# Fills ahead of the counting products, and joined maxima, exponentials, query flips and w2 casts at later steps of the w1 product

## The chip, the core and the metric

One core of a Trainium2 chip runs the kernel. The metric is the device time of one execution in microseconds (us). Inputs and output lie in the chip's memory (HBM).

## The reference

For each of 8 batches, 8 heads attend in two stages: 32 packed queries `p` attend to 576 keys and values, and then the 576 queries `q` attend to the 32 packed rows. The result, 4608 rows of 512, goes through a mixture of 8 experts, of which each row takes the best.

```python
def _attn_ref(q, k, v, p):                       # q, k, v: (8, 8, 576, 64), p: (8, 8, 32, 64)
    p_packed = sm_attn(p, k, v)                  # softmax(p k' / 8) v, with 1e-9 on the sum
    return sm_attn(q, p_packed, p_packed)
...
    logits = xn @ en.T / tau                     # rows and expert embeddings, normalised
    expert_idx = np.argmax(logits, axis=1)
    for e in range(E):                           # w1: (8, 512, 1024), w2: (8, 1024, 512)
        mask = expert_idx == e
        h = np.maximum(x[mask] @ w1[e], 0.0)
        out[mask] = gate_w[mask, None] * (h @ w2[e])
```

## The kernel before

A batch is one unit of work. For the rows of a batch the kernel guesses one expert from the packed rows, runs the two products of that expert for all 576 rows, and counts afterwards whether every row did want it; rows that did not would go through a second part at the end of the program, which these inputs do not enter.

**Two streams are woven by hand.** `ffn(b)` is the expert of batch b and a generator that yields after each group of products on TensorE; a loop at the end of the program (`step_att`) then runs one step of `att_main(b + 1)`, the attention of the next batch. Every engine executes its instructions in the order in which they are written, so a step of the attention stands on each engine behind what `ffn` wrote ahead of the yield and in front of what it writes after it.

**The w1 product** is `hidden(hf, f)`: two halves of the 576 rows (hf) times eight blocks of 128 hidden columns (f), 16 units. Here they are called h0 to h15; h0 to h7 are the first half. Each writes one PSUM bank `pf`, of which there are three, in six products of 128x288, and yields. After the yield its bank is read twice: ScalarE writes the rounded ReLU (L982) and VectorE the remainder (L983, which reads ScalarE's result); in the second half VectorE also copies 64 columns into `h4` (L988). The bank is free when all of these are done, so h(n+3) waits for the readers of h(n). In the second half some units are followed by `split_w2`: a cast of one block of w2 on ScalarE (L886) and the subtraction of its remainder on GpSimd (L887).

**After the w1 product** come eight units of products with `h4` (L1013) and 32 units of the w2 product (L1031), which read `w2s`, the split blocks. With the first step behind the last `h4` unit the attention issues the query scores (L266), which read the four flipped query tiles.

**The attention of batch b+1**, for b+1 from 2 to 7, is `att1`'s `pack()`. Step n stands behind unit n. Before the change:

- Step 0: `counts` of batch b (two products with ones, L824 and L827, and a reduction on VectorE, L829); two fills of parts of the banks for the key scores (L319, VectorE); the key scores on TensorE (L325).
- Steps 1 and 2: `quarter_max` of the two halves of the heads (L337, VectorE).
- Step 3: `whole_max`, six small operations on VectorE (L345 to L351) that join the maxima of four row groups; the first two exponentials (L357, ScalarE).
- Steps 4 to 6: the other six exponentials, two in each. Steps 5 and 7: `quarter_flip`, two additions on GpSimd (L373) and a transpose of 128x640 on VectorE (L374).
- Steps 8 and 9: the first two query flips (L287, VectorE, 128x576).
- Step 12: the values (L384, L393, TensorE). Step 13: sums and scaled rows (L400 to L402, L476, VectorE). Step 14: `pair_turn` (L486, TensorE). Step 15: copy of `x.T` (L550) and the third query flip. Step 16: the fourth. Steps 17 and 18: `row_logits`, `logits_out` (L497, L506).
- Steps 19 to 22: `guess`: products (L610), the index of the largest on VectorE (L616 to L621), and its read by GpSimd, which then issues the loads of w1 and w2. Step 23: the query scores. Then the softmax of the second stage (L656 to L696, mostly VectorE) and `route`, both within the w2 product.
- From unit 18 on a step of `gates` of batch b (L92 to L108 and on, tiny operations of VectorE) follows each step.

**Loads.** Four buffers `nat` hold key and query tiles. A flip of tile i asks for the load of tile i+3; the values' step asks for all keys of the next batch but for those under way. These loads, the values' (`vn`, two buffers) and the stores of the output stand in one queue, that of SyncE, in program order.

Of the kernel before, what the change touches and what calls it, by code (L numbers as in the profile page):

```python
# [27 lines left out]
def kernel(  # L28
# [16 lines left out]
    NG = H // HB  # L45
# [203 lines left out]
    def idle(n):  # L249
        for _ in range(n):  # L250
            yield
# [56 lines left out]
    def area(x, g):  # L308
        t = x.s1[g].rearrange("p (f w) -> p f w", f=2)[:, :, : 2 * QW]
        return t.rearrange("p f (s k) -> p f s k", s=2)  # L310
# [1 line left out]
    def place(h):  # L312
        return h % 2 * 2 + h // 2

    def quarter_scores(x):

        for g in range(NG):
            x.s1[g] = pb.tile([P, 1024], F32, name="pt", tag="pb")
            nc.vector.memset(area(x, g)[64:P, :, :, :32], LOW)  # L319
        for r in range(NPR):  # L320
            for a in range(HB):
                at = RUNS[a] * 32 + (32 if a >= 2 else 0)
                n = QW - (32 if a >= 2 else 0)
                for u in range(2):
                    nc.tensor.matmul(  # L325
                        area(x, r // 2)[32 * a : 32 * a + 32, u, r % 2, QW - n :],
                        half_rows(x.pw, u)[:, r],
                        half_rows(x.kT[r], u)[:, at : at + n],
                        start=True,
                        stop=True,  # L330
                        tile_position=(64 * u, 32 * a),
                    )
# [152 lines left out]
    def pair_turn(x, g, pt):  # L485
        nc.tensor.transpose(  # L486
            pt[:, g * P : (g + 1) * P], pairs_of(x, g), ident
        )

    def pack_tiles(x):  # L490
        x.T = x.Tq = sm.tile([P, NG * P], F32, name="T", tag="T", bufs=1)
        x.ppx = sb.tile([P, NG, XW], F32, name="ppx", tag="ppx", bufs=2)
# [15 lines left out]
    def all_queries(x, nat):  # L508
        for r in range(NPR):
            x.qT[r] = flip(nat(NPR + r))  # L510
            yield

    def att1(x, nat):

        queries = all_queries(x, nat)

        def pack():
            pack_tiles(x)
            quarter_scores(x)
            yield  # L520
            quarter_max(x, 0)
            yield
            quarter_max(x, 1)
            yield
            whole_max(x)
            for g in range(NG):
                for n in range(HB):
                    quarter_exp(x, g, n)
                    if n % 2:
                        yield  # L530
                quarter_flip(x, g)
            yield
            for _ in range(2):
                next(queries)
                yield
            yield from idle(2)
            pt = pb.tile([P, 1024], F32, name="pt", tag="pb")
            sums = pt[:, NG * D : NG * D + NG * QW // 4].rearrange("p (g k) -> p g k", g=NG)
            for g in range(NG):
                quarter_values(x, g, nat(2 * NPR + g), pt[:, g * D : g * D + D], sums[:, g])  # L540
            yield
            quarter_sums(x, sums)
            for g in range(NG):
                pair_rows(x, g, pt[:, g * D : g * D + D])
            yield
            pu = pc.tile([P, 512], F32, name="pu", tag="pu")
            for g in range(NG):
                pair_turn(x, g, pu)
            yield
            nc.vector.tensor_copy(x.T, pu[:, 0 : NG * P])  # L550
            next(queries)
            yield
            next(queries)
            yield
            pt = pc.tile([P, 512], F32, name="pu", tag="pu")
            row_logits(x, pt)
            yield
            logits_out(x, pt)
            yield

        def pack_slowly():
            pack_tiles(x)
            for g in range(NG):
                pt = pb.tile([P, 1024], F32, name="pt", tag="pb")
                p1_turn(x, g, pt)
                yield
                p1_evac(x, g, pt)
                key_sum(x, g)
                yield
            pt = pb.tile([P, 1024], F32, name="pt", tag="pb")  # L570
            for g in range(NG):
                pack_values(x, g, nat(2 * NPR + g), pt[:, g * D : g * D + D])
            yield
            for g in range(NG):
                pair_rows(x, g, pt[:, g * D : g * D + D])
            yield
            pu = pc.tile([P, 512], F32, name="pu", tag="pu")
            yield
            for g in range(NG):
                pair_turn(x, g, pu)  # L580
            yield
            nc.vector.tensor_copy(x.T, pu[:, 0 : NG * P])
            yield
            pt = pc.tile([P, 512], F32, name="pu", tag="pu")
            row_logits(x, pt)
            logits_out(x, pt)
            yield

        if x.halves:
            for g in range(NG):  # L590
                key_max(x, g)
                yield
                key_exp(x, g)
                yield
            yield from pack_slowly()
        else:
            yield from pack()


    def guess(x, late=0, engine=mybir.EngineType.Pool, total=None):  # L600
# [329 lines left out]
    def ffn(x, store, late=False, after=None, end=False, between=None):  # L930
# [30 lines left out]
        def hidden(hf, f):  # L961
            cs = slice(hf * HS, (hf + 1) * HS)
            pf = ps.tile([P, 512], F32, name="pf", tag="pf")

            assert not late or hf == 0 or hf in x.lows and x.gs >= NG * (f // 4 + 1)
            if late and hf == 0:
                ops = [
                    (x.g32[f // 4][:, g, f % 4 * P : f % 4 * P + P], x.ats[0][:, g])
                    for g in range(NG)
                ]  # L970
            else:
                ops = [
                    (x.G[:, a, g, f * P : (f + 1) * P], x.AT[:, m, g, cs])
                    for g in range(NG)
                    for a, m in PASSES
                ]
            for n, (w, r) in enumerate(ops):
                nc.tensor.matmul(pf[:, :HS], w, r, start=(n == 0), stop=(n == len(ops) - 1))  # L978
            yield
            n = HS if hf == 0 else 512 - HS  # L980
            cs = slice(hf * HS, hf * HS + n)
            nc.scalar.activation(hT[:, 0, f, cs], pf[:, :n], AF.Relu)  # L982
            nc.vector.scalar_tensor_tensor(  # L983
                out=hT[:, 1, f, cs], in0=pf[:, :n], scalar=0.0,
                in1=hT[:, 0, f, cs].bitcast(F32), op0=ALU.max, op1=ALU.subtract,
            )
            if hf:
                nc.vector.tensor_scalar(  # L988
                    out=h4[:, f], in0=pf[:, n:HS], scalar1=0.0, scalar2=None, op0=ALU.max
                )  # L990
            if f % 2 and hf and not late:
                split_w2(x)

        if not late and not hasattr(x, "w1g"):
# [86 lines left out]
    def nat_main(b):  # L1081
        def get(i):
            if i < NKQ:
                prefetch(order[b, i] + 3)
                if b > 1 and i in (NPR - 1, NPR):
                    loaded[b, i + NPR + 1] = load_nat(b, i + NPR + 1)
            else:
                prefetch(order[b, NKQ - 1] + 4)
            return loaded[b, i]

        return get

    def att_main(b):
        x = bat[b]
        if b:
            if b > 1:
                counts(bat[b - 1])
            yield from att1(x, nat_main(b))
            sync = b == 1
            queue = nc.sync if sync else nc.gpsimd  # L1100
            yield from guess(
                x, 0 if sync else 2, mybir.EngineType.SP if sync else mybir.EngineType.Pool
            )
            load_w1(x, x.e, queue=queue)
        flips = keys_main(b + 1) if b else None
        second = att2(x, flips, b == 0, b < 1, ENG1 if b == 1 else "vvvvpv")
        if b:
            if b > 1:
                yield
            for _ in range(3 if b == 1 else 2):  # L1110
                yield next(second)
            load_w2(x, x.e, queue)
            if b == 1:
                yield from idle(3)
        yield from second
        x.soft = True
        if b:
            steps = {"r": route(x), "f": flips}
            if b == 1:
                next(flips)  # L1120
            for turn in TURNS:
                for step in turn:
                    next(steps[step], None)
                yield
        if b == B - 1:
            yield from idle(2)
            counts(x)
# [455 lines left out]
```

## Time and profile before

| what | us |
|---|---|
| median of three runs | 448.89 |
| lowest and highest run | 448.1 and 449.75 |
| time of the profiled execution | 449.35 |
| its span | 447.7 |
| TensorE busy | 422.2 |
| VectorE busy | 311.8 |
| ScalarE busy | 198.9 |
| GpSimd busy | 154.8 |

The span is from the first to the last instruction of the profiled execution; 1.65 us of its time lie around it. Matmuls are pipelined and their ends are modelled. In the timelines each line has the start, the length, the engine, the source line, the operation, the tiles and shapes and the number of instructions, and in brackets how long the engine had been idle and what ended that. The chain of waits is followed back from the last instruction.

### The profile page before, as it was taken

The numbers are of one execution on the slowest core, as the hardware profiler recorded it, in microseconds if no ns is written. First come the engines' busy times: TensorE is split into PE (matmuls) and PEld (weight loads), VectorE is DVE, ScalarE is ACT, GpSimd is POOL, SyncE is SP. The second block draws the span as 40 slices with busy tenths as digits, with TensorE's granted clock in tenths as the row PEclk, the third lists the DMA queues.
The fourth block names the chain that finished last, engine by engine and source line by source line (L and its number), as shares of the span: only waits on it lengthen the run. The fifth ranks groups of instructions, "written<-read, shape, count | busy, mean of one in ns | idle before, by whom it ended". The sixth has DMA issues, their size and how long they took to land.

```text
span 447.7 us, 11089 instructions
## 1 busy us (share of the span) xinstructions
PE 422.2 (94%) x4094; PEld 332.0 (74%) x4095; DVE 311.8 (70%) x930; ACT 198.9 (44%) x472; POOL 154.8 (35%) x177
## 2 busy tenths in 40 slices
PE   8899999989998999989999899998999899999993
PEld 5658677777867878678776778777786787769783
DVE  2677686578966789668876779677896588656500
ACT  3567615562264623654146522545236451466210
POOL 2244812445322551425314344034612255142200
PEclk9999999999999999999999999999999999999998
DMA  8899895876978488964979469785698805611012
GB/s 222 293 246 293 229 324 184 223 187 162 378 195 200 99 243 319 226 166 128 294 259 229 123 163 330 240 194 139 185 362 214 198 5 189 243 29 26 14 48 53
DMA packets 42223, 87.92 MB, mean 196 GB/s; under 512 B 11306, under 2 KB 20522, under 8 KB 42162
## 3 DMA queue, kind: packets, MB, share of 16 engines
q1 hardware_dynamic: 34896, 61.44, 51.2%
q0 software_dynamic: 6720, 25.17, 15.5%
q10 hardware_dynamic: 546, 0.54, 0.6%
q8 instruction: 34, 0.56, 0.5%
q14 instruction: 27, 0.22, 0.2%
HBM read 77.68 MB, written 9.44 MB: 195 GB/s over the span
## 4 chain that ended last, share of the span: by engine, by line
PE 86%; DVE 6%; ACT 2%; DMA 2%; issue 1%; SPq 0%; ACTq 0%
PE pf L1031 40%; PE pf L978 21%; PE pf L1013 6%; PE pt L746 5%; PE pt L911 3%; PE pt L266 2%; PE pt L384 2%; PE pt L325 2%; DMA nat<-in_k 2%; DVE hT L983 2%; PE pf L1171 1%; DVE qm L337 1%; ACT p L357 1%; ACT hT L982 1%; PE pu L610 1%
## 5 line engine op out<-in xcount | busy, mean ns | idle before, releaser
L1031 PE MATMUL pf<-w2s,hT 128*128 128x512 f32 (+1 forms) x792 | 183.9, 388 | 0.0
L1031 PEld LDWEIGHTS pf<-w2s,hT 128*128 128x128 f32 x792 | 143.1, 188 | 39.6 <-issue 10.7
L887 POOL TENSOR_TENSOR w2s<-w2r,w2s 128x512 fp32r<-128x512 f32 x64 | 81.6, 1286 | 121.3 <-ACT w2s L886 61.2
L978 PE MATMUL pf<-AT,G 128*128 128x288 f32 x720 | 109.9, 302 | 10.9 <-DVE hT L983 9.6
L978 PEld LDWEIGHTS pf<-AT,G 128*128 128x128 f32 x720 | 98.2, 188 | 20.2 <-DVE hT L983 13.4
L983 DVE SCALAR_TENSOR_TENSOR hT<-pf,hT 128x224 fp32r<-128x224 f32 (+1 forms) x128 | 52.5, 412 | 32.3 <-ACT hT L982 30.8
L982 ACT ACTIVATE hT<-pf 128x224 fp32r<-128x224 f32 (+1 forms) x128 | 49.5, 392 | 56.4 <-PE pf L978 55.1
L1372 ACT ACTIVATE o<-pf,gate 128x512 f32<-128x512 f32 (+1 forms) x41 | 25.9, 633 | 35.3 <-PE pf L1031 21.9
L886 ACT CAST w2s<-w2r 128x512 fp32r<-128x512 f32 x64 | 38.6, 616 | 0.0
L287 DVE STREAM_TRANSPOSE kt<-nat 128x576 f32<-128x576 f32 x52 | 37.9, 756 | 0.2 <-issue 0.2
L758 ACT ACTIVATE scr<-pt 128x512 f32<-128x512 f32 (+2 forms) x47 | 24.9, 531 | 24.7 <-PE pt L746 23.8
L1013 PE MATMUL pf<-w2r,h 128*64 128x256 f32 x256 | 33.8, 388 | 0.0
L373 POOL TENSOR_TENSOR qs<-p 128x320 f32<-128x320 f32 x12 | 10.6, 881 | 50.5 <-ACT p L357 50.5
L761 DVE TENSOR_REDUCE lg<-pt 128x8 f32<-128x32 f32 (+2 forms) x47 | 8.6, 182 | 27.7 <-ACT scr L758 27.5
L670 ACT ACTIVATE st<-st 128x576 f32<-128x576 f32 (+1 forms) x17 | 11.1, 658 | 34.4 <-DVE st L667 32.6
L746 PEld LDWEIGHTS pt<-ppx,at 64*128 64x128 f32 (+1 forms) x320 | 19.4, 175 | 7.1 <-issue 4.6
L746 PE MATMUL pt<-ppx,at 64*128 64x136 f32 (+1 forms) x320 | 24.3, 290 | 0.0
L696 POOL TENSOR_TENSOR AT<-at,AT 128x576 fp32r<-128x576 f32 x7 | 10.0, 1423 | 40.4 <-ACT AT L691 40.4
L1013 PEld LDWEIGHTS pf<-w2r,h 128*64 128x64 f32 x256 | 19.4, 137 | 4.9 <-issue 1.8
L357 ACT ACTIVATE p<-pt,qnm 128x160 f32<-128x160 f32 x48 | 16.9, 424 | 12.0 <-DVE qnm L351 12.0
L691 ACT CAST AT<-at 128x576 fp32r<-128x576 f32 x15 | 10.1, 674 | 22.7 <-DVE at L685 22.7
L849 ACT ACTIVATE lg<-lg 128x40 f32<-128x40 f32 x8 | 1.9, 237 | 40.8 <-DVE lg L845 40.8
(205 smaller groups left out, 484.2 us busy)
## 6 DMA issues: line engine op xcount, KB each, us to landing
nat<-in_q SPq DMA_DIRECT2D x112, 140.0 KB, 3.3
nat<-in_k SPq DMA_DIRECT2D x96, 140.0 KB, 2.9
w1t<-in_moe_w POOLq DMA_DIRECT2D x12, 1024.0 KB, 9.2
w2r<-in_moe_w POOLq DMA_DIRECT2D x24, 512.0 KB, 11.8
out<-o SPq DMA_DIRECT2D x124, 64.0 KB, 2.7
vn<-in_v SPq DMA_DIRECT2D x48, 160.0 KB, 4.2
w2r<-in_moe_w SPq DMA_DIRECT2D x8, 512.0 KB, 9.8
nat<-in_k SPq DMA_DIRECT2D x4, 576.0 KB, 7.2
```

The costliest lines, as they stand in the source:

```text
L287: nc.vector.transpose(kt.rearrange("p (c i) -> p c i", i=32), t)
L357: nc.scalar.activation(x.p1[g][:, n * QW : n * QW + QW], area(x, g)[:, n // 2, n % 2], AF.Exp, bias=x.nm[:, at : at + 1],)
L746: nc.tensor.matmul(to[: rows(c), half], x.at[at, g, c * P : c * P + rows(c)], x.ppx[at, g], start=True, stop=True, tile_position=(64 * hal ...
L758: nc.scalar.activation(scr[:r, :, : pt.shape[2]], pt[:r, :, :, : 2 * D], AF.Square, accum_out=sss[:r])
L886: nc.scalar.copy(t[:, 0], raw)
L887: nc.gpsimd.tensor_tensor(out=t[:, 1], in0=raw, in1=t[:, 0].bitcast(F32), op=ALU.subtract)
L978: nc.tensor.matmul(pf[:, :HS], w, r, start=(n == 0), stop=(n == len(ops) - 1))
L982: nc.scalar.activation(hT[:, 0, f, cs], pf[:, :n], AF.Relu)
L983: nc.vector.scalar_tensor_tensor(out=hT[:, 1, f, cs], in0=pf[:, :n], scalar=0.0, in1=hT[:, 0, f, cs].bitcast(F32), op0=ALU.max, op1=ALU.su ...
L1013: nc.tensor.matmul(pf[64 * hf : 64 * hf + 64, :256], h4[:, f], x.w2r[f // 2][:, f % 2, hf * 256 : hf * 256 + 256], start=(f == 0), stop=(f ...
L1031: nc.tensor.matmul(pf[:, :w], hT[:, a, f, c * P : (c + 1) * P], x.w2s[f][:, m, at : at + w], start=(f == 0 and i == 0), stop=(f == NF - 1 ...
L1372: nc.scalar.activation(o[:, :w], pf[:, :w], AF.Copy, scale=x.gate[:, c : c + 1])
```

## The change

The two fills move out of `quarter_scores` into `quarter_banks`, which is called ahead of `counts`. `whole_max` moves from step 3 to step 4, and two more empty steps follow it, so that the exponentials stand at steps 6 to 9 and the `quarter_flip` parts at steps 8 and 10. The four query flips stand at steps 12 (behind the values), 14, 18 (behind `logits_out`) and 20 (behind `guess`'s index). Of `split_w2` the four calls in the second half follow f = 4 to 7 (h12 to h15) instead of f = 1, 3, 5, 7 (h9, h11, h13, h15). The loads of the two value tiles are asked for by the third and fourth key flip instead of the fourth key flip and the first query flip. The step numbers of values, sums, `pair_turn`, copy, logits, guess and query scores stay.

```diff
-    def quarter_scores(x):
-
+    def quarter_banks(x):
         for g in range(NG):
             x.s1[g] = pb.tile([P, 1024], F32, name="pt", tag="pb")
             nc.vector.memset(area(x, g)[64:P, :, :, :32], LOW)
+
+    def quarter_scores(x):
...
-    def att1(x, nat):
-
-        queries = all_queries(x, nat)
-
-        def pack():
+    def att1(x, nat, queries=None):
+
+        def pack(queries):
             pack_tiles(x)
+            if not x.s1:
+                quarter_banks(x)
             quarter_scores(x)
             yield
-            quarter_max(x, 0)
-            yield
-            quarter_max(x, 1)
+            for g in range(NG):
+                quarter_max(x, g)
+                yield
             yield
             whole_max(x)
+            yield from idle(2)
             for g in range(NG):
                 for n in range(HB):
                     quarter_exp(x, g, n)
                     if n % 2:
                         yield
                 quarter_flip(x, g)
-            yield
-            for _ in range(2):
-                next(queries)
-                yield
             yield from idle(2)
...
                 quarter_values(x, g, nat(2 * NPR + g), pt[:, g * D : g * D + D], sums[:, g])
+            next(queries)
             yield
             quarter_sums(x, sums)
...
                 pair_turn(x, g, pu)
+            next(queries)
             yield
             nc.vector.tensor_copy(x.T, pu[:, 0 : NG * P])
-            next(queries)
-            yield
-            next(queries)
-            yield
+            yield from idle(2)
             pt = pc.tile([P, 512], F32, name="pu", tag="pu")
             row_logits(x, pt)
             yield
             logits_out(x, pt)
+            next(queries)
             yield
...
-            yield from pack()
+            asked = queries or all_queries(x, nat)
+            yield from pack(asked)
+            if queries is None:
+                drain(asked)
...
-            if f % 2 and hf and not late:
+            if f >= 4 and hf and not late:
                 split_w2(x)
...
-                if b > 1 and i in (NPR - 1, NPR):
-                    loaded[b, i + NPR + 1] = load_nat(b, i + NPR + 1)
+                if b > 1 and i in (NPR - 2, NPR - 1):
+                    loaded[b, i + NPR + 2] = load_nat(b, i + NPR + 2)
...
             if b > 1:
+                quarter_banks(x)
                 counts(bat[b - 1])
-            yield from att1(x, nat_main(b))
+            queries = all_queries(x, nat_main(b)) if b > 1 else None
+            yield from att1(x, nat_main(b), queries)
...
-            yield from guess(
+            for n, _ in enumerate(guess(
                 x, 0 if sync else 2, mybir.EngineType.SP if sync else mybir.EngineType.Pool
-            )
+            )):
+                if n == 1 and queries:
+                    next(queries)
+                yield
```

## Rows read from the trace of the kernel before

**Rows 1.** The page's busy times of the engines, with shares and instructions.
```profile
PE 422.2 (94%) x4094; PEld 332.0 (74%) x4095; DVE 311.8 (70%) x930; ACT 198.9 (44%) x472; POOL 154.8 (35%) x177
```
**Rows 2.** Chain of waits, whole run: start, length, engine, tile, line, instructions.
```profile
84.46 0.79 PE pf L978 x6
...
104.40 1.01 PE pf L1013 x8
...
295.87 0.79 PE pf L978 x6
...
315.81 1.01 PE pf L1013 x8
320.13 1.13 PE pt L266 x32
...
348.71 0.79 PE pf L978 x6
...
368.66 1.01 PE pf L1013 x8
...
402.06 12.71 PE pf L978 x96
```
**Rows 3.** Timeline of TensorE from 295 us: where it stood idle in one w1 product.
```profile
297.51 1.29 PE L325 MATMUL pt<-kt,pw 64*32 64x160 f32 x64 [0.57 <-DVE pt L319]
...
304.54 7.01 PE L978 MATMUL pf<-AT,G 128*128 128x288 f32 x42 [1.59 <-DVE hT L983]
```
**Rows 4.** Timeline of ScalarE, same stretch: the exponentials and a w2 cast.
```profile
303.01 0.68 ACT L357 ACTIVATE p<-pt,qnm 128x160 f32<-128x160 f32 x2 [2.00 <-DVE qnm L351]
...
308.66 0.61 ACT L886 CAST w2s<-w2r 128x512 fp32r<-128x512 f32 x1
```
**Rows 5.** Timeline of VectorE, same stretch: fills, joined maxima, flips, sums, logits, index.
```profile
297.20 0.30 DVE L319 MEMSET pt<- 64x128 f32 x2
...
301.85 0.17 DVE L345 COPY qlow<-qm 64x8 f32<-64x8 f32 x1
...
302.82 0.16 DVE L351 COPY qnm<-qnm 64x8 f32<-64x8 f32 x1
304.02 0.46 DVE L983 SCALAR_TENSOR_TENSOR hT<-pf,hT 128x288 fp32r<-128x288 f32 x1 [1.04 <-ACT hT L982]
...
305.27 0.83 DVE L374 STREAM_TRANSPOSE p1T<-p 128x640 f32<-128x640 f32 x1
...
308.10 0.76 DVE L287 STREAM_TRANSPOSE kt<-nat 128x576 f32<-128x576 f32 x1
...
313.07 0.24 DVE L400 TENSOR_REDUCE qr<-pt 128x2 f32<-128x80 f32 x1 [0.58 <-PE pt L393]
...
317.77 0.14 DVE L506 COPY ppx<-pu 128x16 f32<-128x16 f32 x1
317.82 0.27 DVE L92 TENSOR_SCALAR rq_i<-ss 128x5 int32<-128x5 int32 x1
...
319.51 0.22 DVE L621 TENSOR_SCALAR sel<-ecol,gi 1x8 f32<-1x8 f32 x1
```
**Rows 6.** Timelines of GpSimd (w2 subtractions, two stretches), then of VectorE in the second.
```profile
316.78 1.28 POOL L887 TENSOR_TENSOR w2s<-w2r,w2s 128x512 fp32r<-128x512 f32 x1 [0.52 <-ACT w2s L886]
...
343.19 2.51 POOL L887 TENSOR_TENSOR w2s<-w2r,w2s 128x512 fp32r<-128x512 f32 x2 [10.28 <-ACT w2s L886]
...
344.55 1.20 DVE L809 SCALAR_TENSOR_TENSOR oh<-lg,code 128x40 f32<-128x40 f32 x1
```
**Rows 7.** Single lines of VectorE, whole run: shortest, median and longest in ns.
```profile
L92 DVE TENSOR_SCALAR rq_i<-ss x8: 153/268/270, 57.1 to 415.6; 128x5 int32<-128x5 int32 x8
L401 DVE TENSOR_SCALAR qr<-qr x6: 168/169/170, 101.9 to 366.2; 128x2 f32<-128x2 f32 x6
L809 DVE SCALAR_TENSOR_TENSOR oh<-lg,code x8: 199/1198/1203, 55.8 to 397.4; 128x40 f32<-128x40 f32 x8
```
**Rows 8.** Timelines of VectorE, then TensorE, within the w2 product that follows.
```profile
329.71 0.78 DVE L685 STREAM_TRANSPOSE at<-st 128x576 f32<-128x576 f32 x1
...
332.98 1.20 PE L746 MATMUL pt<-ppx,at 64*128 64x136 f32 x16
```
**Rows 9.** Timeline of SyncE's queue: the last three key loads of the next batch.
```profile
313.78 7.84 SPq L194 DMA_DIRECT2D nat<-in_k  x12
```

## The prediction

> **What bounds the kernel now.** I read the page's busy times first: TensorE is busy for 422 of 447.7 us [rows 1], so the change can only win by closing the rest, and the question is where the rest lies. The chain of waits answers that. In six batches the attention of the next batch runs beside the w1 product, and h0 to h15 with its steps take from 295.87 to 315.81, 19.94 us; the first and the last of the six take 19.94 and 19.95 [rows 2]. The last batch has no attention beside it, and its sixteen units take 12.71 us, 0.79 each [rows 2]. The difference, 7.2 us, is not all idle time: key scores, values, counts and the turn are TensorE's own work. So I went to TensorE's timeline for the idle time proper [rows 3]. It shows three losses in each of the six products:
>
> - 0.57 us in front of the key scores, which wait for the fills. VectorE does them at 297.20 [rows 5], behind the reduction of the counts, which itself waits for TensorE.
> - 1.59 us in front of h6 at 304.54 [rows 3], ended by the remainder of h3 on VectorE at 304.02, which had waited 1.04 us for ScalarE [rows 5]. ScalarE had stood 2.00 us in front of the first exponentials, waiting for the joined maxima [rows 4], with the ReLU of h3 queued behind them. That is the whole chain: maxima, six joins from 301.85 to 302.98 [rows 5], two exponentials of 0.68 us, ReLU, remainder, bank, h6.
> - h6 to h12, 42 products, take 7.01 us [rows 3] where seven units at 0.79 take 5.53: 1.48 us in small pieces. VectorE is the cause: from 305.27 two transposes of 128x640 and two query flips (0.83 and 0.76 each [rows 5]) stand one after another between the remainders, and each remainder releases its bank late.
>
> Together 3.64 us in each of six products, 21.8 us in all. That is what there is to gain; a little under 5%.
>
> **Fills ahead of the counts.** They cost VectorE the same 0.30 us [rows 5], but now between the last reading of the previous banks and h0's readers, when VectorE waits for TensorE anyway. The key scores follow the counts at once: minus 0.57.
>
> **Joined maxima at step 4, exponentials from step 6.** I walk the engines in order, each instruction starting when its engine and its inputs are free, with durations from the rows, and with h0 at the same time as before. With the scores 0.57 earlier, h1 starts at 298.2 and h2 to h6 follow each other at 0.79, h6 at 302.2, because ScalarE no longer waits in front of h3's ReLU and h3's bank is free at 301.8. But the joins, 1.15 us, now stand in front of h4's remainder: they run from 301.7 to 302.8, h4's bank comes free at 303.4, and h7, which could start at 303.0, starts 0.40 late. The exponentials find their maxima ready. So 1.59 goes and 0.40 comes.
>
> **Transposes at steps 8 and 10, query flips at 12, 14, 18 and 20.** VectorE now has in steps 5 to 11 eight remainders and two transposes and no query flip. In the walk only h11 still starts late, by 0.08. The values need the second transpose and the sums of GpSimd; both are ready at 307.9 and TensorE comes there at 308.2. So 1.48 goes and 0.08 comes. The first flip stands beside the values, the second beside h14 and h15, when VectorE has some room: no bank is late for them in the walk. Their shift by up to four steps costs in itself nothing, since the query scores are at step 23, except for the last two, below.
>
> **The casts behind h12 to h15.** ScalarE then spends 0.36 on the ReLU and about 0.55 on each cast (0.61 long, [rows 4]), 0.9 a unit, while TensorE has values and turn between the units: no loss there. But the four subtractions on GpSimd at 1.28 us each [rows 6] now run almost without a break from 309.4 to 310.7 and 311.6 to 315.5, and end some 2.7 us behind h15, where before the last ended at 318.06, 2.3 us behind it. w2's blocks are read from about 318 on, so TensorE doesn't wait for them.
>
> VectorE may. Its first `gates` operation at 317.82 took 0.27 us and ended with the subtraction at 318.06 [rows 5, 6]; its shortest is 0.15 [rows 7]. L809, with two inputs in SBUF, took 1.20 us beside the subtractions from 343.19 to 345.70 [rows 6], against 0.20 at shortest [rows 7]. So an operation of this kind that meets a subtraction waits until its end. Two places meet one. First, L401 in the sums, 0.17 us in all six batches [rows 7] because GpSimd happened to rest there; in the walk it comes at 310.0 and the subtraction ends at 310.7. The scaled rows are ready 0.5 later, at 311.5, and `pair_turn`, which TensorE reaches at 311.2, comes 0.30 late. Bounds: 0 (no wait) and 1.28 (a whole subtraction); I take 0.30. The second place is the next step.
>
> The Trainium skill's page "SBUF — State Buffer", section "Who interferes with whom", says the same as a rule: a VectorE instruction with two SBUF inputs contends with a GpSimd instruction that reads SBUF, and whichever came first holds the shared ports for its whole length. By that rule L401, with one tensor input, waits only if it runs in a two-port mode; L92, of the same form, did wait here. If it does not, each batch gains 0.30 more and the time would be 433.2.
>
> **The last two query flips.** This is the new wait that I expect. Before, all flips were done ahead of `logits_out` at 317.77 [rows 5], 2.4 us ahead of the query scores at 320.13 [rows 2]. After, `logits_out` starts when the logits are there, about 1.4 us behind h15; then come the third flip (0.7), six `gates` operations (six at about 0.2), the index (0.8, ending with L621), and only then the fourth flip (0.76). That is 4.9 us behind h15. TensorE is ready for the query scores 4.32 us behind h15 (320.13 less 315.81 [rows 2]) and needs the fourth tile some 0.4 us later. So 0.1 to 0.2 are lost if nothing else happens, and up to 0.6 if the first `gates` operation meets the last subtraction (which ends at 315.5, where the operation comes at about 315.0). I take 0.5. Bounds: 0 and, if two of the six each wait out a subtraction, about 2.
>
> Further behind, VectorE is late against TensorE by another 0.7 us or so. The turn of the first half ends at 330.49 before and the row products want it at 332.98 [rows 8], so 2.5 us of slack cover this.
>
> **Loads.** The value loads stand one flip earlier in SyncE's queue and both of their buffers are free by then; free. The key loads of the next batch wait for the flips: the last three are under way from 313.78 to 321.62 [rows 9], and would end at about 320, with the first stores behind them. Nobody waits for either before the key flips some 15 us later.
>
> **The sum.** In each of six products: 0.57 + 1.59 + 1.48 goes, 3.64; 0.40 + 0.08 + 0.30 + 0.50 comes, 1.28. Net 2.36, times six 14.2 us. The w2 product behind is TensorE's own time and keeps its length. The profiled execution took 449.35 (span 447.7 and 1.65 around it): 435.2 after. It lies 0.46 above the median of the runs, so by the median it is 434.7. I say 435.0.
>
> **The rivals.**
> 1. GpSimd and VectorE do not meet, and each operation keeps its shortest time: then 3.64 less 0.48, and at most 0.15 for the fourth flip, is 3.0 a product, 18 us: 431. For it: the meeting hangs on tenths of a us. Against: subtractions fill most of 309 to 315.5. 0.17.
> 2. VectorE remains the bound: it was busy without a break for the seven units, and the transposes still follow each other. If half of 1.48 stays and the fourth flip costs 1.0 rather than 0.5, the gain is 1.1 a product, 7 us: 442. For it: the walk leaves margins of only 0.1 to 0.4 us at h9 to h12. 0.14.
> 3. The change doesn't do what it says: the banks stay late for another reason (h4 behind the joins instead of h3 behind the exponentials), and what h6 to h12 won is lost ahead of the query scores. Then only the fills' 0.57 is left, partly: within 2 us of 449. 0.05.
> 4. Slower: the fourth flip behind `gates`. Of the six tiny operations five have two SBUF inputs or the form of L92. If each of four waits out a subtraction (1.2 instead of 0.2, as L809 did), the flip ends 4.0 us later, the query scores wait 4.2, and with 3.1 won in front each product loses 1.1: 456. It decides where the subtractions run past h15 by more than about 6 us, so that more than three operations meet one. Against: in the walk only the last one is still running then. 0.05.
>
> **How the numbers follow.** The forecast, 432.5 to 438.5, has 0.59; rivals 1 and 2 have 0.17 and 0.14, 3 and 4 have 0.05 each. The range takes in 1 and most of 2: 429 to 442. What a measurement of this kernel can tell from no change is about 0.5%, 2.2 us. Faster by more than that are the forecast and rivals 1 and 2, 0.90, less 0.01 of rival 2's tail; within are rival 3 and that tail, 0.05; slower is rival 4 and 0.01 of what I have not thought of.
>
> **What would show it.** In the chain of waits after, h0 to h15 with their steps should take about 17.1 us instead of 19.94. TensorE should show no idle time in front of the key scores, a few tenths in front of h7, none in front of h6, and some tenths in front of `pair_turn` and within the query scores, ended by VectorE's L476 and L287. L401 should be longer than 0.17, and ScalarE should not wait for the joined maxima. The prediction is wrong if h6 to h12 still take 7 us, or if the query scores stand more than 1 us behind the last `h4` product.

## The result, and the profile after

| kernel | median us | ratio to the kernel before | 95% interval |
|---|---|---|---|
| before, beside it | 449.32 | 1 | |
| after | 436.56 | 0.9721 | 0.9687 to 0.9756 |

The time fell by 2.8%. The prediction said 435.0, within 429.0 to 442.0. The profiled execution after took 436.40 with a span of 434.8.

The page of the changed kernel: the busy line that answers [rows 1], the group of the w1 product, and the chain's shares.

```profile
PE 418.2 (96%) x4094; PEld 330.1 (76%) x4095; DVE 319.1 (73%) x930; ACT 200.2 (46%) x472; POOL 154.0 (35%) x177
...
PE 75%; DVE 13%; DMA 3%; SPq 3%; ACT 2%; issue 2%; DVEq 0%; ACTq 0%
...
L979 PE MATMUL pf<-AT,G 128*128 128x288 f32 x720 | 104.8, 299 | 1.8 <-DVE hT L984 1.7
```

TensorE now does the same 4094 instructions in a span 12.9 us shorter. Line numbers have moved by one or a few: L979 is the old L978, L326 the old L325, L984 the old L983, L888 the old L887, L402 the old L401 and L622 the old L621.

The timeline of TensorE after, for the fifth w1 product with attention beside it, which answers [rows 3] and the same product in [rows 2] (start, length, engine, line, shape, number, and in brackets the idle time):

```profile
286.57 0.95 PE L979 MATMUL pf<-AT,G 128*128 128x288 f32 x6
...
287.63 1.28 PE L326 MATMUL pt<-kt,pw 64*32 64x160 f32 x62
288.83 5.01 PE L979 MATMUL pf<-AT,G 128*128 128x288 f32 x36
294.13 5.13 PE L979 MATMUL pf<-AT,G 128*128 128x288 f32 x36 [0.29 <-DVE hT L984]
...
303.51 1.08 PE L1014 MATMUL pf<-w2r,h 128*64 128x256 f32 x8
...
307.57 0.70 PE L266 MATMUL pt<-kt,T 64*32 64x288 f32 x12
308.91 1.16 PE L266 MATMUL pt<-kt,T 64*32 64x288 f32 x20 [0.64 <-DVE rq_t L105]
310.00 5.28 PE L1032 MATMUL pf<-w2s,hT 128*128 128x512 f32 x22
```

Of the three losses of before, the first is gone: no idle time stands in front of the key scores. The second has shrunk from 1.59 to 0.29 and moved from h6 to h7. Of the third little is left: h7 to h12, the second group of 36, take 5.13. A new one has come: the query scores (L266) stop after 12 of their 32 products and go on at 308.91.

To compare kernels I use two stretches of this batch, both from TensorE's timeline: A from the start of h0 to the first `h4` product, B from there to the first w2 product. Before they are 20.03 (295.71 to 315.74) and 5.45 (to 321.19); after, 16.94 and 6.49. So A gives 3.09 and B takes back 1.04: 2.05 a batch, 12.3 in six. In the other five batches A and B are the same to within 0.03, before and after. The rest of the 12.9 lies ahead of the first of the six, where nothing was changed, and in the tail: the first h0 starts at 83.55 after and at 84.46 before, 0.9 us, less 0.35 at the end. That start differs as much without any edit: two measurements of one kernel below have it at 83.53 and 85.10.

The flips that the query scores wait for, in the timeline of VectorE after:

```profile
301.07 0.48 DVE L402 TENSOR_SCALAR qr<-qr 128x2 f32<-128x2 f32 x1
...
304.82 0.17 DVE L507 COPY ppx<-pu 128x16 f32<-128x16 f32 x1
305.00 0.78 DVE L287 STREAM_TRANSPOSE kt<-nat 128x576 f32<-128x576 f32 x1
305.70 0.78 DVE L92 TENSOR_SCALAR rq_i<-ss 128x5 int32<-128x5 int32 x1
...
307.90 0.22 DVE L622 TENSOR_SCALAR sel<-ecol,gi 1x8 f32<-1x8 f32 x1
308.08 0.78 DVE L287 STREAM_TRANSPOSE kt<-nat 128x576 f32<-128x576 f32 x1
```

and GpSimd beside it:

```profile
300.24 1.28 POOL L888 TENSOR_TENSOR w2s<-w2r,w2s 128x512 fp32r<-128x512 f32 x1 [1.59 <-ACT w2s L887]
302.70 3.76 POOL L888 TENSOR_TENSOR w2s<-w2r,w2s 128x512 fp32r<-128x512 f32 x3 [1.17 <-PE pu L487]
```

The fourth flip ends at 308.86, and the query scores go on at 308.91. The profile names L105 as the releaser, a tiny operation that starts at 308.78 and writes nothing that the scores read; the flip is the one that they read. Two small operations ahead of the fourth flip have grown: L402 from 0.17 to 0.48, ending at 301.55 where the subtraction ends at 301.52, and L92 from 0.27 to 0.78, ending at 306.48 where the three subtractions end at 306.46.

The chain of waits after gives another account of the stop (start, length, what):

```profile
303.29 1.70 DMA pn<-in_p
304.99 0.01 issue
305.00 0.78 DVE kt L287
305.78 0.70 DVE rq_i L92
...
308.08 0.78 DVE kt L287
308.86 0.06 DVE rq_t L105
308.91 1.16 PE pt L266 x20
```

It leads from the flips back to a load of packed rows. That is the rival to my account: the third flip waits for a transfer, and its place does not matter.

### The profile page after: what moved, and what is told of

It is laid out like the page before. It is cut to its first block, busy times and chain, and to the rows that moved or that the text cites. A ratio compares the mean times of both kernels' runs of the same rounds, so it can differ in the third digit from the quotient of the medians.

```text
span 434.8 us, 11089 instructions
## 1 busy us (share of the span) xinstructions
PE 418.2 (96%) x4094; PEld 330.1 (76%) x4095; DVE 319.1 (73%) x930; ACT 200.2 (46%) x472; POOL 154.0 (35%) x177
## 4 chain that ended last, share of the span: by engine, by line
PE 75%; DVE 13%; DMA 3%; SPq 3%; ACT 2%; issue 2%; DVEq 0%; ACTq 0%
PE pf L1032 41%; PE pf L979 14%; PE pt L747 5%; PE pt L912 3%; DVE hT L984 3%; DVE kt L287 3%; PE pf L1014 2%; PE pt L266 2%; DMA pn<-in_p 2%; PE pt L326 2%; SPq L194 1%; DVE p1T L375 1%; PE pf L1177 1%; ACT hT L983 1%; SPq L233 1%
## 5 line engine op out<-in xcount | busy, mean ns | idle before, releaser
L1032 PEld LDWEIGHTS pf<-w2s,hT 128*128 128x128 f32 x792 | 143.1, 188 | 39.6 <-issue 10.7
L888 POOL TENSOR_TENSOR w2s<-w2r,w2s 128x512 fp32r<-128x512 f32 x64 | 80.8, 1284 | 107.8 <-ACT w2s L887 73.6
L979 PE MATMUL pf<-AT,G 128*128 128x288 f32 x720 | 104.8, 299 | 1.8 <-DVE hT L984 1.7
L979 PEld LDWEIGHTS pf<-AT,G 128*128 128x128 f32 x720 | 97.8, 188 | 6.4 <-DVE hT L984 3.9
L983 ACT ACTIVATE hT<-pf 128x224 fp32r<-128x224 f32 (+1 forms) x128 | 49.4, 386 | 48.3 <-PE pf L979 47.2
L984 DVE SCALAR_TENSOR_TENSOR hT<-pf,hT 128x224 fp32r<-128x224 f32 (+1 forms) x128 | 52.2, 413 | 21.0 <-ACT hT L983 20.4
L887 ACT CAST w2s<-w2r 128x512 fp32r<-128x512 f32 x64 | 38.6, 616 | 0.0
L877 POOL DMA_DIRECT2D w2r<-in_moe_w x24 | 16.9, 711 | 0.0
```

The lines of the kernel that those rows point to most:

```text
L877: queue.dma_start(t, w2e[:, 2 * i : 2 * i + 2, :])
L887: nc.scalar.copy(t[:, 0], raw)
L888: nc.gpsimd.tensor_tensor(out=t[:, 1], in0=raw, in1=t[:, 0].bitcast(F32), op=ALU.subtract)
L984: nc.vector.scalar_tensor_tensor(out=hT[:, 1, f, cs], in0=pf[:, :n], scalar=0.0, in1=hT[:, 0, f, cs].bitcast(F32), op0=ALU.max, op1=ALU.su ...
L1032: nc.tensor.matmul(pf[:, :w], hT[:, a, f, c * P : (c + 1) * P], x.w2s[f][:, m, at : at + w], start=(f == 0 and i == 0), stop=(f == NF - 1 ...
```

## The experiments

The theory has four statements: (1) the fills cost what they idle TensorE; (2) the early exponentials hold ScalarE, and with it h3's bank and h6; (3) query flips among h8 to h12 make banks late; (4) the last two flips wait in their new place, behind `gates` and the index, which themselves wait for GpSimd's subtractions.

All kernels, with stretches A and B of the same batch (the fifth of the six). The other five agree with it to within 0.07 in A and 0.03 in B, except that with gates from 20 (both times) and with joins split B is 5.20 in the other five:

| kernel | median us | ratio, 95% interval | A | B |
|---|---|---|---|---|
| before | 447.9 to 449.3 | 1 | 20.03 | 5.45 |
| after | 436.56 | 0.972 (0.969 to 0.976) | 16.94 | 6.49 |
| fills only | 443.90 | 0.991 (0.987 to 0.994) | 19.27 | 5.46 |
| flips as before | 436.46 | 0.972 (0.969 to 0.975) | 17.89 | 5.42 |
| exponentials as before | 447.27 | 0.996 (0.994 to 0.998) | 18.70 | 6.48 |
| flips at 16 and 18 | 428.88 | 0.956 (0.953 to 0.959) | 16.93 | 5.20 |
| gates from 20 | 428.18 | 0.954 (0.952 to 0.957) | 16.94 | 5.33 |
| the same again | 428.58 | 0.956 (0.953 to 0.958) | 16.94 | 5.33 |
| casts at odd f | 434.41 | 0.969 (0.966 to 0.973) | 17.26 | 5.87 |
| joins split, gates from 20 | 430.41 | 0.960 (0.956 to 0.964) | 17.17 | 5.34 |
| casts later, gates from 20 | 434.33 | 0.969 (0.966 to 0.971) | 16.88 | 6.08 |

**Fills only.** The kernel before, with `quarter_banks` ahead of `counts`.

```diff
             if b > 1:
+                quarter_banks(x)
                 counts(bat[b - 1])
```

> The kernel before with one part of the change: the two fills ahead of the counts. Theory (the key scores waited 0.57 us for the fills in each of six w1 products, and nothing behind takes this back): 6 x 0.57 = 3.4 us less, about 445.9 where before is 449.3. Rival (h6 waits for h3's remainder anyway, so what is won in front is lost there): no change, 449. It decides by the start of h6 against h0.

443.9, 4.4 us less than the kernel before beside it (448.3). A is 0.76 shorter, more than the 0.57 that the timeline gave as idle; by the starts of lines the key scores stand 1.80 behind h0 before and 1.04 after (292.59 less 291.55). The whole gain arrives at the end of the product: h6 waits as long as before for h3's remainder, but it does so earlier. The timeline of TensorE in this kernel:

```profile
291.55 0.95 PE L981 MATMUL pf<-AT,G 128*128 128x288 f32 x6
...
292.59 0.33 PE L326 MATMUL pt<-kt,pw 64*32 64x160 f32 x2
...
299.63 7.01 PE L981 MATMUL pf<-AT,G 128*128 128x288 f32 x42 [1.59 <-DVE hT L986]
```

The rival, that the wait at h6 would swallow it, falls: the chain of h6 starts with the key scores, so it moves with them.

**Exponentials as before.** The changed kernel with maxima, exponentials and transposes at their old steps.

```diff
-            yield
             whole_max(x)
-            yield from idle(2)
...
-            yield from idle(2)
+            yield from idle(5)
```

> The changed kernel with the joined maxima at step 3 and exponentials and transposes at steps 3 to 7 as before; fills, late query flips and casts stay. Theory (ScalarE stands in front of the first exponentials until the maxima are joined, h3's ReLU behind it, and h6 waits 1.6 us): the wait comes back, with the transposes among h5 to h8 partly as well; h0 to h15 take about 18.7 us instead of 16.9, 11 us more in six, 447. Rival (the late query flips and the casts made most of the gain): 440 or less.

447.27, 10.7 us more than the changed kernel, with A at 18.70 (18.7 forecast) and B at 6.48. The wait at h6 is back in full, in TensorE's waits (who waited for whom, total, times, longest) and timeline:

```profile
PE pf L977 <- DVE hT L982: 9.6, 6, 1.6
PE pt L266 <- DVE rq_t L105: 3.8, 6, 0.6
...
303.83 6.37 PE L977 MATMUL pf<-AT,G 128*128 128x288 f32 x42 [1.60 <-DVE hT L982]
```

The second line shows that the stop in the query scores is there as well. So statement 2 holds, and it is the largest part of the change: without it, fills, late flips and casts together are worth 1.3 us (447.27 against 448.56 beside it). The edit moves joins, exponentials and transposes together; that the exponentials are what holds h6 is read from the wait, as in the prediction, and no run moves them alone. Statement 3 agrees with it: h6 to h12 take 6.37 here, with the two transposes but no query flip among them, and 7.01 with both [rows 3].

**Flips as before.** The changed kernel with the query flips at steps 8, 9, 15 and 16.

```diff
                     if n % 2:
+                        if g:
+                            next(queries)
                         yield
...
             nc.vector.tensor_copy(x.T, pu[:, 0 : NG * P])
-            yield from idle(2)
+            next(queries)
+            yield
+            next(queries)
+            yield
```

> The changed kernel with the four query flips back at steps 8, 9, 15 and 16. Theory (late flips win about 1.0 us within h8 to h12, where they stood between the remainders, and lose about 1.0 us in front of the query scores): the two cancel, 436.6 within 2 us; h0 to h15 take about 17.9 us instead of 16.9, and the stretch from h15 to the w2 product 5.45 instead of 6.47. Rival (the flips are what held h8 to h12, and the wait in front of the query scores comes from a transfer and stays): slower, 442 or more.

436.46 against 436.56: the late flips, as the change places them, are worth nothing. A is 17.89 and B 5.42, so the 0.95 that they win among the hidden units is what they lose in front of the w2 product. The wait that they had removed is in TensorE's timeline at h11:

```profile
295.38 3.46 PE L981 MATMUL pf<-AT,G 128*128 128x288 f32 x24 [0.29 <-DVE hT L986]
299.35 2.12 PE L981 MATMUL pf<-AT,G 128*128 128x288 f32 x12 [0.51 <-DVE h L991]
...
310.00 1.20 PE L266 MATMUL pt<-kt,T 64*32 64x288 f32 x32
311.13 5.05 PE L1034 MATMUL pf<-w2s,hT 128*128 128x512 f32 x21
```

The query scores run unbroken here, 32 in one piece. This alone does not decide against a transfer, because each flip also asks for a load, so the edit moves loads in SyncE's queue as well.

**Flips at steps 16 and 18.** The changed kernel; the third and fourth flip stand ahead of all `gates` operations and of the index.

```diff
             nc.vector.tensor_copy(x.T, pu[:, 0 : NG * P])
-            yield from idle(2)
+            yield
+            next(queries)
+            yield
...
-                if n == 1 and queries:
-                    next(queries)
```

> The changed kernel with the third query flip at step 16 (ahead of the logits' copy) and the fourth at step 18 (behind it), so that both stand ahead of the gates' operations and the index. Theory (the query scores wait for the fourth flip because it stands behind them): the wait of 0.92 us and the broken row of query products go, about 1.3 us in each of six, 7.5 us less than the changed kernel, 429. Rival (the chain of waits names the transfer of the packed rows and SyncE's queue in front of the third flip, so the flips wait for data): no gain, 436.5.

428.88, 7.7 us less than the changed kernel. B falls from 6.49 to 5.20, 1.29 in each of six, which is all of it. TensorE in this kernel:

```profile
298.54 1.08 PE L1016 MATMUL pf<-w2r,h 128*64 128x256 f32 x8
...
302.60 1.20 PE L266 MATMUL pt<-kt,T 64*32 64x288 f32 x32
303.74 2.56 PE L1034 MATMUL pf<-w2s,hT 128*128 128x512 f32 x10
```

**Gates from unit 20 on.** The changed kernel with one constant altered; the flips stay where the change put them.

```diff
-    GATE = 18
+    GATE = 20
```

> The changed kernel with the gates' operations two steps later (from unit 20 on), so that none of them stands in front of the index and the fourth flip; the flips stay. Theory (six small operations, the first of them held by GpSimd's subtraction to 0.76 us, delay the fourth flip by 1.7 us): the wait in front of the query scores falls from 0.92 us to 0.1 or less, 429 to 431. Rival (a transfer): no gain, 436.5. A loss by later gates (the first store waits for them on ScalarE) would show as an idle TensorE in the w2 product.

428.18, and 428.58 in a second measurement. Flips, their loads and SyncE's queue are those of the changed kernel; only six tiny operations no longer stand in front. VectorE in this kernel:

```profile
301.58 0.22 DVE L622 TENSOR_SCALAR sel<-ecol,gi 1x8 f32<-1x8 f32 x1
301.75 0.78 DVE L287 STREAM_TRANSPOSE kt<-nat 128x576 f32<-128x576 f32 x1
302.46 0.13 DVE L92 TENSOR_SCALAR rq_i<-ss 128x5 int32<-128x5 int32 x1
```

and TensorE:

```profile
302.41 1.34 PE L266 MATMUL pt<-kt,T 64*32 64x288 f32 x32
303.68 8.70 PE L1032 MATMUL pf<-w2s,hT 128*128 128x512 f32 x37
```

The flip ends 0.12 behind the start of the scores, and there is no stop; the 32 products take 1.27 to the w2 product here instead of 1.13, and B is 5.33. In the other five batches the index comes 0.2 earlier and B is 5.20, as with the flips at 16 and 18; the second measurement has the same. With this and the kernel before it, the account of the chain of waits (the transfer of packed rows) falls, and statement 4 stands. The first store does wait longer for the gates on ScalarE, 11.3 us in all instead of 6.4, and none of TensorE's waits is for it. Of the second measurement was expected:

> The kernel with the gates' operations from unit 20 on once more, beside the one with later casts on the same chip: 428.2 by the first measurement.

**Casts at odd f.** The changed kernel with the w2 casts behind h9, h11, h13 and h15.

```diff
-            if f >= 4 and hf and not late:
+            if f % 2 and hf and not late:
```

> The changed kernel with the four w2 casts back behind h9, h11, h13 and h15, two of their subtractions thus 2 us or more earlier on GpSimd. Theory (L402 in the sums, 0.48 us after the change and 0.17 before, and the first gates operation, 0.76 and 0.27, wait for the subtraction that runs on GpSimd): L92 falls to 0.3 or less, since the last subtraction then ends at about the time it starts; the query scores wait 0.5 us less in each of six, 3 us. Against it stands the subtraction behind h9, which now comes ahead of the second group's additions on GpSimd; the values may wait up to 0.4 us for them. Together 432 to 436. Rival (the two operations are long for another reason, as late operands): L402 and L92 keep 0.48 and 0.76, and the time 436.5.

434.41, 2.1 us less than the changed kernel and within the 432 to 436 expected. L92 falls to 0.16 because it starts at 304.97 now, almost when the last subtraction ends (305.10); B is 0.62 shorter, where 0.5 was expected. A is 0.32 longer, where up to 0.4 was. The intervals of the two times overlap, but all six batches show both differences, together 1.8 us. GpSimd shows why A is longer:

```profile
296.81 1.30 POOL L888 TENSOR_TENSOR w2s<-w2r,w2s 128x512 fp32r<-128x512 f32 x1 [1.11 <-ACT w2s L887]
298.06 0.89 POOL L374 TENSOR_TENSOR qs<-p 128x320 f32<-128x320 f32 x1
299.02 0.53 POOL L374 TENSOR_TENSOR qs<-qs 128x160 f32<-128x160 f32 x1
299.50 1.29 POOL L888 TENSOR_TENSOR w2s<-w2r,w2s 128x512 fp32r<-128x512 f32 x1
```

The subtraction behind h9 stands in front of the second group's additions, which the values need, and the next one, to 300.79, holds L402: it takes 0.59 here (300.23 to 300.82), more than in the changed kernel. So moving the casts to the end was right for the values, and both operations do follow the subtraction that happens to run. In the change as it stands, though, it cost more at the fourth flip than it won at the values.

**Joins split.** Gates from 20, and the six joining operations split between steps 4 and 5.

```diff
         nc.vector.tensor_tensor(out=low, in0=x.qm[:64], in1=low, op=ALU.min)
+        yield
...
-            whole_max(x)
-            yield from idle(2)
+            yield from whole_max(x)
+            yield
```

> The changed kernel with the gates' operations from unit 20 on, and the six joining operations split: two at step 4, four at step 5. Theory (h7 waits 0.3 us because all six stand in front of h4's remainder, 1.15 us in one piece): the wait in front of h7 goes and 0.1 to 0.2 at h9 may come, as the exponentials start 0.4 later; 427 where the kernel with later gates alone took 428.2. Rival (VectorE has no room at all there and the wait moves to h8 or h9 in full): 428.2.

430.41, about 2 us more than with later gates alone (428.18 and 428.58). Its runs overlap with those of the second measurement, but A is 0.23 longer in all six batches, 1.4 us. The wait in front of h7 is gone, but 0.18 is idle in front of h11, released by the `h4` copy of h8:

```profile
293.70 1.82 PE L980 MATMUL pf<-AT,G 128*128 128x288 f32 x12 [0.18 <-DVE h L990]
```

The exponentials, 0.4 later, push h6's ReLU, the transpose and all remainders behind it. My theory was wrong here. The rival was right that the wait only moves, and even it expected no loss. It is not VectorE by itself that is full: it stands 0.56 and 0.41 idle there, waiting for ReLUs on ScalarE. The two engines' readers of the banks together have no room from h4 to h11, so what is taken off one unit is given to another.

**Casts later.** Gates from 20, and the casts behind h13, h14 and twice behind h15, so that GpSimd rests during the sums.

```diff
-            if f >= 4 and hf and not late:
+            if f >= 5 and hf and not late:
                 split_w2(x)
+                if f == NF - 1:
+                    split_w2(x)
```

> The changed kernel with the gates' operations from unit 20 on, and the four w2 casts one place later: behind h13, h14 and twice behind h15, so that GpSimd subtracts nothing while the sums run. Theory (L402 takes 0.48 instead of 0.17 us because it waits for the subtraction behind h12, and TensorE's turn stands behind it): L402 falls to 0.17, the stretch from h0 to h15 gets 0.2 to 0.3 us shorter in each of six, 1.2 to 1.8 us; 426.5 where the kernel with later gates alone gives 428.2. Rival (the turn is late for another reason, the values' end): L402 falls, the time stays at 428.2.

434.33, 5.7 us more than the kernel without this edit beside it (428.58). L402 did fall to 0.17 in all six, and A became 0.06 shorter, not 0.2 to 0.3: for the turn the rival was right. But B grew by 0.75 in this batch and by 0.88 in the other five, together with A 4.8 us. The 0.9 left over is no more than the start of the first h0 varies. VectorE and GpSimd in this kernel:

```profile
304.04 0.14 DVE L620 CAST gi<-idx 1x1 f32<-1x1 uint32 x1
304.21 1.02 DVE L622 TENSOR_SCALAR sel<-ecol,gi 1x8 f32<-1x8 f32 x1
305.15 0.76 DVE L287 STREAM_TRANSPOSE kt<-nat 128x576 f32<-128x576 f32 x1
```

```profile
300.21 5.00 POOL L888 TENSOR_TENSOR w2s<-w2r,w2s 128x512 fp32r<-128x512 f32 x4 [4.05 <-PE pu L487]
```

L622, eight numbers on one partition, took 1.02 us instead of 0.22 (1.22 to 1.23 in the other five). It ended at 305.23, when the fourth subtraction ended (305.21), and the fourth flip behind it was late again: the scores go on at 305.97 instead of unbroken. I had freed one small operation from the subtractions and put them onto another that TensorE does wait for.

## Why the prediction was right, and where its terms were off

**What there is to gain.** Right: TensorE's idle time in six products, and the three places. The change doesn't touch the w2 product behind them; from its start to the next h0 it takes 27.36 us in both kernels by the starts in the timelines.

**Fills.** The mechanism was right, the size low: 0.57 forecast, 0.76 measured in stretch A of the kernel with the fills only. I had taken the idle time in the bracket. Matmul ends are modelled and overlap, so the distance from h0 to the scores, 1.80 less 1.04, was the better reading.

**Joined maxima and exponentials.** Right. 1.59 goes at h6, and the joins cost at h7, 0.40 forecast and 0.29 measured. The kernel with the old steps shows that this part carries the change.

**Query flips out of the hidden units.** Right for what they win: 0.95 in A, by undoing them. My term was 1.48 for transposes and flips together and only 0.08 left behind; h7 to h12 still take 5.13 for six units of 0.79, about 0.4 more. Part of that is the modelled tail of the last product, which the 7.01 of before contains as well. By difference from A (3.09 less 0.76 and 1.59, plus 0.29 and 0.06) transposes and flips gave 1.09 where the terms said 1.40.

**L402 and the turn.** L402 is the prediction's L401. The wait came as forecast, 0.3 us longer and ended by the subtraction. Its price did not: 0.30 forecast, 0.06 by the kernel in which L402 is short. TensorE reached the turn at 302.35, where the scaled rows were ready at 302.40; in the walk it stood there 0.3 earlier. A wait was priced at its length, without asking how late TensorE itself would be.

**The last two flips.** The mechanism was right in each step: third flip, first `gates` operation held to the end of the last subtraction, five more, the index, the fourth flip, 5.35 us behind the first `h4` product (4.9 forecast, and up to 0.5 more by the subtraction). The price was too low, 0.5 forecast against 1.04. Two errors partly cancel. I let the twelve products that need no fourth tile count as 0.42 us of work done; but the other twenty then took 1.09 from 308.91 to the w2 product, where all 32 take 1.13 unbroken [rows 2]. The head start was worth next to nothing; the last section shows why. On the other side, TensorE came to the query scores 0.26 sooner behind h15, 4.06 us instead of 4.32, because `logits_out` no longer stood behind two flips and the guess no longer waited for it; I had kept 4.32. Nor was it the subtraction alone that decided between 0.1 to 0.2 and 0.5: with the casts at odd f no small operation is held in front of the fourth flip, and B still loses 0.42; with later gates it loses nothing. The prediction had named as a sign of being wrong that the query scores stand more than 1 us behind the last `h4` product. Twelve of them start at once, the other twenty 1.34 behind the first: for these the sign was there.

**The sum.** 2.36 net in each batch forecast, 2.05 measured: A gave 3.09 where the terms said 2.86, B took 1.04 where they said 0.50. In six that is 14.2 and 12.3. That A came so close is partly luck: fills, joins and turn came out 0.54 better than forecast, transposes and flips 0.31 worse. That the time came within 1.6 us of 435.0 is no finer test of the terms, since the start of the first h0 alone varies by as much. The rule of the Trainium skill's page "SBUF — State Buffer", section "Who interferes with whom", agrees with these traces: L402, L92 and L622 each end within 0.03 us of the subtraction that they met. That L402 and L622 have one tensor input and wait all the same fits the two-port clause of that rule (L622 also takes the number it compares with from a tile, `gi`); no run here shows the mode itself.

**The loads.** The earlier value loads were put at nothing. No run takes them out alone; neither before nor after does TensorE wait for a value tile in the six products.

**The rivals.** That GpSimd and VectorE do not meet fell with L402 and L92. That VectorE stays the bound was half right: with ScalarE it has no room from h4 to h11, but at much less cost. "Slower" had the right place, the fourth flip behind small operations, and the wrong count: one of them met a subtraction, not four (and all six have one of the two forms, not five). Casting one unit later made one meet again, at the same place, for 5.7 us.

## What to carry to other kernels

When an instruction waits on its engine, the cost is what stands behind it in that engine's order: here a ReLU behind an exponential, then a remainder, a bank and a product. Move the waiting instruction behind the work that others need, and then look at what it was moved in front of or behind: the flips of this change won 0.95 and lost 1.04 until a constant took six tiny operations out of their way, and with that the gain was 4.4 to 4.6% instead of 2.8%. Before placing small VectorE operations on a path that TensorE waits for, look at what GpSimd runs at that moment, in both orders of the edit.

## What the runs showed of the hardware that I had not expected

A broken row of small matmuls can lose its head start. The 32 query products (64x32 weights, 288 columns) take 1.13 us in one piece from 320.06 to 321.19. Stopped after twelve, the remaining twenty took 1.09 from their restart, in the changed kernel (308.91 to 310.00) and in the one with later casts (305.97 to 307.06):

```profile
305.04 0.70 PE L266 MATMUL pt<-kt,T 64*32 64x288 f32 x12
305.97 1.16 PE L266 MATMUL pt<-kt,T 64*32 64x288 f32 x20 [0.22 <-DVE kt L287]
```

I had reckoned in proportion, 0.71. The starts of the single products in the traces show why. `rounds` in the kernel gives each product one of eight positions on the array (`tile_position`), four products to each. Unbroken, the 32 start as four eights, 0.24 to 0.27 us apart: all positions side by side, and in each one product behind the other. The twelve start as two sixes; none of them is in the two positions that work on the fourth tile. Behind the restart come eight, eight, two and two, again 0.24 to 0.27 apart. So six positions had half of their work behind them, but two had all four products left, and the row lasts as long as its fullest position. All six batches show the same starts.

An operation on eight numbers can take nearly as long as one on 128x512 of another engine. L622 took 0.22 us with GpSimd free and 1.02 beside its subtractions, while a conversion of one number, L620, took 0.14 in the middle of the same subtraction (304.04, subtractions from 300.21 to 305.21). So not every small VectorE operation waits; the tensor-scalar forms L92, L402 and L622 did, the conversion and the transposes did not. Nor did a tensor-scalar form that reads PSUM, the `h4` copy L989: in the changed kernel it takes 0.20 to 0.22 us, within a subtraction as well as away from them.
